# Feed-forward matmuls moved from column tiles to the four quadrants of TensorE, beside attention that already runs there

## The chip, the cores and the metric

One core of one Trainium2 chip. In the profiles PE is TensorE and PEld its weight loads, ACT is ScalarE, DVE VectorE, POOL GpSimd, SP SyncE, and SPq the queue of SP. Results of PE lie in banks of PSUM; an *eviction* is the instruction by which another engine takes one out of there. The metric is the device time of one execution in microseconds (us). A kernel's time is the median of its runs. A ratio of two kernels is computed from the mean time of one kernel's fast runs over the mean time of the other's fast runs of the same rounds, so it is not quite the ratio of the medians that are quoted. "Fast" and "slow" are states of a run: on one core, a run more than 1.5% above the fastest run of the same kernel is called slow.

## The reference

Sigmoid attention over 8 batches, 12 heads, 448 positions and head size 64, then a feed-forward block with SiLU on the 3584 x 768 result (768 to 2048 to 768). Cut to what matters:

```python
scores = scale * np.matmul(q, k.transpose(0, 1, 3, 2)) - np.log(S)
attn = 1.0 / (1.0 + np.exp(-scores))
x = np.matmul(attn, v)            # heads side by side: (8 * 448, 768)
h = x @ w_in                      # 768 -> 2048
g = h * (1.0 / (1.0 + np.exp(-h)))
out = g @ w_out                   # 2048 -> 768
```

## The kernel before

Attention has a contraction of 64 (head size, or 64 keys) and outputs of 64 rows, so it runs in the four 64x64 quadrants of TensorE. One *score step* is four such matmuls of 448 columns, followed by a sigmoid on ACT. The *values* of four heads are 28 of them. The feed-forward products have a contraction of 128 and run as two 128x64 column tiles. I call the matmuls that use the whole array once a *round*: four quadrant matmuls, or two column-tile matmuls. Attention of batch b+1 is woven into the feed-forward stream of batch b, a few score steps at each *visit*. Batch 0 has no feed-forward work to go with it; the last batch's feed-forward work has no attention left.

The parts that matter (cuts marked `# ...`):

```python
ps_sc = ctx.enter_context(tc.tile_pool(name="ps_sc", bufs=2, space=bass.MemoryType.PSUM))  # scores: two pairs of banks
ps_1 = ctx.enter_context(tc.tile_pool(name="ps_1", bufs=4, space=bass.MemoryType.PSUM))    # all else: four single banks

def matmul2(ps, lhsT, rhs, start, stop):          # 128x64 column tiles
    for i in range(2):
        nc.tensor.matmul(ps[half(i)], lhsT[:, half(i)], rhs, start=start, stop=stop)

def scores(b, i, r):                              # 64x64 quadrants
    # ...
    psc = ps_sc.tile([P, 2, 512], F32, tag="pssc", name=f"psc_{b}_{i}_{r}")
    for t in range(2):
        for j in range(2):
            nc.tensor.matmul(
                psc[half(j), t, :S], kT[half(t), r, half(j)], qT[half(t), :, half(j)],
                start=True, stop=True,
            )
    return nc.scalar.activation(attn[b, i][:, :, r, :], psc[:, :, :S], AF.Sigmoid, bias=bias_s, scale=QKSCALE)

def h_unit(b, fc):                                # one 128-row block of h
    # ...
    for cc in range(NCC):
        matmul2(ph[:, :S], w_in_sb[:, cc, fc * P : (fc + 1) * P], xTs[b][:, cc, :], cc == 0, cc == NCC - 1)
    # sigmoid on ACT, product on DVE

# the driver: visits of two or three score steps
while n < len(steps) or waiting:
    now = waiting[:]
    visit = steps[n : n + (3 if now else 2)]
    acts = [scores(*s) for s in visit[:2]]
    for quad in now:
        values(*quad)
    # ...
    gemm(stream_at(n) if n < len(steps) else 1e9 if not waiting else stream_at(n - 0.5))
```

## Time and profile before

| | before |
|---|---|
| median of 3 runs | 401.49 us (401.16 to 403.14) |
| span of the profiled run, granted clock | 399.4 us, 1.00 |
| TensorE (PE) busy | 390.3 us, 98% |
| first feed-forward round starts | 29.1 us |

The first lines of the page of the kernel before follow: busy time by engine, then the span in 40 slices, in tenths busy (PE) and in tenths of the full clock (PEclk), and the chain of waits by engine.

```profile
span 399.4 us, 11191 instructions
PE 390.3 (98%) x5020; PEld 229.7 (58%) x5020; DVE 152.2 (38%) x254; ACT 223.2 (56%) x298; POOL 55.3 (14%) x69
...
PE   8999998999999999999999999999999999999995
...
PEclk9999999999999999999999999999999999999999
...
PE 88%; DMA 9%; POOL 1%; ACT 0%; SPq 0%; issue 0%; DVE 0%; POOLq 0%
```

PE bounds this kernel: it is busy everywhere at full clock, and the chain of waits is 88% PE. But a busy PE is not a PE at its peak. One visit in the timeline of PE shows it (start us, duration us, engine, line, operation, tile, shapes, count; L179 is the score step, L248 the output product):

```profile
162.37 0.38 PE L179 MATMUL psc_2_6_2951<-qT_2_1954,kT_2_1958 64*64 64x448 f16 x4
162.58 0.36 PE L179 MATMUL psc_0_0_2958<-qT_0_2469,kT_0_2473 64*64 64x448 f16 x4
162.87 2.79 PE L248 MATMUL po_0_2969<-w_out_sb,gT_2357 128*64 128x384 f16 x32
165.59 0.38 PE L179 MATMUL psc_0_1_3003<-qT_0_2469,kT_0_2473 64*64 64x448 f16 x4
```

Read the starts, not the durations, because matmuls overlap. The starts of consecutive rounds inside a product are 0.189 us apart with 448 columns and 0.1625 us with 384 columns. The two score steps and 16 output rounds from 162.37 to 165.59 ought to take 2 x 0.189 + 16 x 0.1625 = 2.98 us, and took 3.22. The missing 0.24 us lie at the two borders: 0.10 us going in, 0.10 us coming out, and 0.025 us in the first round after each. The Trainium skill ("TensorEngine Tiling (Array Packing)", Key Properties) says that changing the tiling mode, not just the tile, drains TensorE. This trace agrees: gaps stand where 64x64 and 128x64 tiles meet, and none between score steps and values, which are both 64x64.

Summed over the whole stream, from 29.1 us to PE's end, the rounds take 347.1 us and PE loses 18.2 us: 12.1 us at the borders, 3.1 us in the slower first rounds, 2.0 us in one wait for a DMA, and about 1 us in small pieces.

### The profile page before, as it was taken

Reading aid. Unit: us, or ns where it says so; the run is one execution under the profiler, and the core shown is the slowest. Engines: PE = TensorE matmul, PEld = TensorE weight load, DVE = VectorE, ACT = ScalarE, POOL = GpSimd, SP = SyncE. Lnnn points to the kernel's source line nnn. Section 1 sums busy time; section 2 is a strip of 40 time slices with the busy share of each in tenths; the row PEclk is TensorE's granted clock in tenths of the full one; section 3 lists DMA queues with packets and bytes.
Section 4 is the critical chain, followed back from the end, with each engine's and each line's share of the span. In section 5 each row is a group of like instructions: output and inputs, shape, how many; then the busy total and the mean of one; then the engine's idle time right before and its main releaser. Section 6 shows DMA issues by size and latency. Waiting matters only on the chain.

```text
span 399.4 us, 11191 instructions
## 1 busy us (share of the span) xinstructions
PE 390.3 (98%) x5020; PEld 229.7 (58%) x5020; DVE 152.2 (38%) x254; ACT 223.2 (56%) x298; POOL 55.3 (14%) x69
## 2 busy tenths in 40 slices
PE   8999998999999999999999999999999999999995
PEld 4565554555665556655566555555566555665663
DVE  3544632244323542235322443235421454235411
ACT  2998764477534874566634775467634578214200
POOL 3642020123202110122002120021100000000000
PEclk9999999999999999999999999999999999999999
DMA  7999999699928881595135981396713100130033
GB/s 258 259 252 232 217 218 157 158 172 311 214 56 191 199 178 36 140 240 158 36 80 141 229 173 25 94 217 174 122 41 81 41 2 2 41 80 2 2 80 79
DMA packets 64655, 53.80 MB, mean 135 GB/s; under 512 B 35424, under 2 KB 61024, under 8 KB 64608
## 3 DMA queue, kind: packets, MB, share of 16 engines
q1 hardware_dynamic: 50976, 41.30, 41.5%
q0 software_dynamic: 13632, 11.80, 19.6%
q8 instruction: 39, 0.64, 0.6%
q14 instruction: 8, 0.07, 0.0%
HBM read 45.61 MB, written 11.01 MB: 142 GB/s over the span
## 4 chain that ended last, share of the span: by engine, by line
PE 88%; DMA 9%; POOL 1%; ACT 0%; SPq 0%; issue 0%; DVE 0%; POOLq 0%
DMA kT_0_1135<-xk_0_1133 3%; DMA stk_0_1015<-in_k_dram 2%; DMA v_0_140<-in_v_dram 2%; DMA stk_0_83<-in_k_dram 1%; PE po_0_6030 L248 1%; PE po_0_3461 L248 1%; PE po_1_3055 L248 1%; PE po_0_2869 L248 1%; PE po_0_2748 L248 1%; PE po_1_2321 L248 1%; PE po_0_2147 L248 1%; PE po_0_5909 L248 1%; PE po_0_5788 L248 1%; PE po_1_5393 L248 1%; PE po_1_5259 L248 1%; PE po_0_5225 L248 1%
## 5 line engine op out<-in xcount | busy, mean ns | idle before, releaser
L84 PEld LDWEIGHTS <-w_in_sb 128*64 128x64 f16 x1536 | 84.3, 110 | 63.6 <-issue 10.7
L248 PEld LDWEIGHTS <-gT_3896 128*64 128x64 f16 x224 | 14.0, 110 | 7.7 <-issue 1.8
L248 PEld LDWEIGHTS <-gT_2357 128*64 128x64 f16 x224 | 14.0, 110 | 7.7 <-issue 1.8
L248 PEld LDWEIGHTS <-gT_724 128*64 128x64 f16 x224 | 13.9, 110 | 7.8 <-issue 2.0
L248 PEld LDWEIGHTS <-gT_5429 128*64 128x64 f16 x224 | 14.1, 110 | 7.0 <-issue 0.9
L248 PEld LDWEIGHTS <-gT_1552 128*64 128x64 f16 x224 | 14.0, 110 | 5.8 <-issue 1.4
L248 PEld LDWEIGHTS <-gT_4630 128*64 128x64 f16 x224 | 14.0, 110 | 5.8 <-issue 1.4
L248 PEld LDWEIGHTS <-gT_3091 128*64 128x64 f16 x224 | 14.0, 110 | 5.8 <-issue 1.4
L248 PEld LDWEIGHTS <-gT_6100 128*64 128x64 f16 x224 | 14.4, 110 | 4.7
L92 PEld LDWEIGHTS <-zeros 64*64 64x64 f16 x180 | 6.3, 121 | 4.3 <-issue 1.9
L92 PE MATMUL pz_start<-zeros 64*64 64x448 f16 x44 | 4.3, 577 | 1.2 <-DVE bias_s L67 1.2
L102 POOL DMA_DIRECT2D w_in_sb<-in_moe_w_in_dram x8 | 5.3, 670 | 0.0
L133 POOL DMA_DIRECT2D v_6_3858<-in_v_dram x1 | 0.8, 821 | 27.9 <-PE psc_0_3_3852 L179 27.9
L183 ACT ACTIVATE attnT_0_197<-psc_0_0_198,bias_s 128x896 f16<-128x896 f32 x1 | 1.0, 1007 | 6.3 <-PE psc_0_0_198 L179 6.3
L233 ACT ACTIVATE tsig_0_6114<-ph_0_6101 128x448 f16<-128x448 f32 x1 | 0.5, 545 | 6.9 <-PE ph_0_6101 L84 6.9
L200 PEld LDWEIGHTS <-v_0_140 64*64 64x64 f16 x84 | 2.8, 106 | 2.0 <-DMA v_0_140<-in_v_dram 1.1
L133 POOL DMA_DIRECT2D v_5_3053<-in_v_dram x1 | 0.8, 821 | 22.5 <-PE psc_0_3_3047 L179 22.5
L133 POOL DMA_DIRECT2D v_7_4592<-in_v_dram x1 | 0.8, 821 | 22.5 <-PE psc_0_3_4586 L179 22.5
L183 ACT ACTIVATE attnT_2_5764<-psc_2_4_5926,bias_s 128x896 f16<-128x896 f32 x1 | 1.0, 1008 | 4.5 <-PE psc_2_4_5926 L179 4.5
L183 ACT ACTIVATE attnT_2_4255<-psc_2_4_4425,bias_s 128x896 f16<-128x896 f32 x1 | 1.0, 1007 | 4.5 <-PE psc_2_4_4425 L179 4.5
L183 ACT ACTIVATE attnT_2_3484<-psc_2_4_3673,bias_s 128x896 f16<-128x896 f32 x1 | 1.0, 1008 | 4.5 <-PE psc_2_4_3673 L179 4.5
L183 ACT ACTIVATE attnT_2_2716<-psc_2_4_2886,bias_s 128x896 f16<-128x896 f32 x1 | 1.0, 1007 | 4.5 <-PE psc_2_4_2886 L179 4.5
(1084 smaller groups left out, 986.8 us busy)
## 6 DMA issues: line engine op xcount, KB each, us to landing
w_in_sb<-in_moe_w_in_dram POOLq DMA_DIRECT2D x8, 384.0 KB, 11.3
w_out_sb<-in_moe_w_out_dram POOLq DMA_DIRECT2D x2, 1536.0 KB, 24.4
v_0_140<-in_v_dram POOLq DMA_DIRECT2D x3, 224.0 KB, 7.9
v_1_456<-in_v_dram POOLq DMA_DIRECT2D x1, 672.0 KB, 16.4
v_2_1204<-in_v_dram POOLq DMA_DIRECT2D x1, 672.0 KB, 16.8
v_3_1514<-in_v_dram POOLq DMA_DIRECT2D x1, 672.0 KB, 8.1
v_4_2319<-in_v_dram POOLq DMA_DIRECT2D x1, 672.0 KB, 10.0
v_5_3053<-in_v_dram POOLq DMA_DIRECT2D x1, 672.0 KB, 7.2
```

Source lines behind the costliest of these rows:

```text
L84: nc.tensor.matmul(ps[half(i)], lhsT[:, half(i)], rhs, start=start, stop=stop)
L92: nc.tensor.matmul(pz[j][half(t), :S], zeros[half(j), :D], zeros[half(j)], start=True, stop=True)
L102: nc.gpsimd.dma_start(w_in_sb[half(t), :, f], moe_w_in[t * NCC * D : (t + 1) * NCC * D, f].rearrange("(c d) f -> d c f", d=D),)
L133: nc.gpsimd.dma_start(v16s[b].rearrange("p t i f -> p (t i) f"), src.rearrange("p t i f -> p (t i) f"))
L183: return nc.scalar.activation(attn[b, i][:, :, r, :], psc[:, :, :S], AF.Sigmoid, bias=bias_s, scale=QKSCALE)
L200: nc.tensor.matmul(pav[j][half(t), :S], v16s[b][half(j), t, i, r * D : (r + 1) * D], attnT[half(j), t, r, :], start=(r == 0), stop=(r == R ...
L233: nc.scalar.activation(tsig, ph[:, :S], AF.Sigmoid, bias=0.0, scale=ISX)
L248: nc.tensor.matmul(po[half(s), :NO2], gTs[bl][:, fc, r * D : (r + 1) * D], w_out_sb[:, fc, e], start=(fc == 0), stop=(fc == NFC - 1),)
```

## The change

The intent: run the feed-forward products in the four quadrants too, so that TensorE never changes mode while there is attention to do. A contraction of 128 is then split over the two row halves of the array. Two row halves may not write the same PSUM bank at the same time: the Trainium skill says so ("TensorEngine Tiling (Array Packing)", Gotcha 1: PSUM Pressure). So two products are made at once, in a pair of banks. In the first phase row half 0 adds to bank 0 and row half 1 to bank 1; in the second phase they change over. Between the phases all matmuls of the first must have ended. A no-op on SP's queue waits for them and PE waits for the no-op; one score step is put there to cover the time. The array time of two products stays the same.

PSUM is dealt out anew: one pair of banks for scores (before: two), three pairs for everything else; in batch 0 alone every second score takes a pair of the others. Evictions become twice as wide. The q and k transposes of batches 0 and 1 share one tile. Score steps come one at a time, so there are more, shorter visits.

The diff, cut to its core:

```diff
-    ps_sc = ctx.enter_context(tc.tile_pool(name="ps_sc", bufs=2, space=bass.MemoryType.PSUM))
-    ps_1 = ctx.enter_context(tc.tile_pool(name="ps_1", bufs=4, space=bass.MemoryType.PSUM))
+    ps_sc = ctx.enter_context(tc.tile_pool(name="ps_sc", bufs=1, space=bass.MemoryType.PSUM))
+    ps_2 = ctx.enter_context(tc.tile_pool(name="ps_2", bufs=3, space=bass.MemoryType.PSUM))
 ... (cut)
-    def transpose_pe(b: int, i: int, nm: str, cuts=(0, R)):
+    def transpose_pe(b: int, i: int, cuts=(0, R), between=None):
+        ptr = ps_2.tile([P, 2, 1024], F16, tag="ps2", name=f"ptr_{b}_{i}")
+        for n, nm in enumerate("qk"):
 ... (cut: transposes into ptr[:, n], eviction by DVE)
+    def products(n, nk, lhs, rhs, out_of):
+        if attending[0]:
+            for ph in range(2):
+                for k in range(nk):
+                    for row in range(2):
+                        u = row ^ ph
+                        for c in range(2):
+                            mm = nc.tensor.matmul(
+                                out_of(u)[half(c)],
+                                lhs(u, k, c)[half(row)],
+                                rhs(u, k)[half(row)],
+                                start=(ph == 0 and k == 0),
+                                stop=(ph == 1 and k == nk - 1),
+                            )
+                            if ph == 1 and k == row == c == 0:
+                                tc.add_manual_dep(
+                                    mm.ins, change.ins.name, AFTER, reason="rows change over"
+                                )
+                    if ph == 0 and k == nk - 1:
+                        change = nc.sync.nop()
+                        tc.add_manual_dep(
+                            change.ins, mm.ins.name, AFTER, reason="rows change over"
+                        )
+                        for dma in stores:
+                            dma()
+                        stores.clear()
+                    yield n, (ph * nk + k + 1) / (2 * nk)
+        else:
 ... (cut: 128x64 column tiles as before, for the last batch)
+        if kind == "h":
+            o_pairs, o_done = 0, 0
+            if share == 0.5:
+                attend()          # one score step at the change-over
+            o_quota = min((b + 1) * NQ * R + AHEAD, len(steps) + 1) - done
+        elif share < 1 and (done < len(steps) or waiting or share == 0.5):
+            progress = (o_pairs + share) / len(tiles_of(b))
+            if share == 0.5 or o_done < o_quota * progress - 0.5:
+                attend()          # in output pairs: at the change-over, and wherever behind the quota
+                o_done += 1
```

More of the change, by code (lines that the diff above doesn't have):

```diff
@@ L1 @@
+import itertools
 import math
 from contextlib import ExitStack
+from functools import partial
 import concourse.bass as bass
@@ L79, in half, with ps_tile @@
         return slice(i * D, (i + 1) * D)
-    def matmul2(ps, lhsT, rhs, start, stop):
-        for i in range(2):
-            nc.tensor.matmul(ps[half(i)], lhsT[:, half(i)], rhs, start=start, stop=stop)
+    def ps_tile(name, pool=None, tag="ps2"):
+        return (pool or ps_2).tile([P, 2, 512], F32, tag=tag, name=name)
     def idle(n: int, key: str):
-        pz = [ps_1.tile([P, 512], F32, tag="ps1", name=f"pz{i}_{key}") for i in range(2)]
+        pz = ps_tile(f"pz_{key}")
         for _ in range(n):
@@ L92, in idle @@
                     nc.tensor.matmul(
-                        pz[j][half(t), :S], zeros[half(j), :D], zeros[half(j)], start=True, stop=True
+                        pz[half(t), j, :S], zeros[half(j), :D], zeros[half(j)], start=True, stop=True
                     )
@@ L157, in transpose_dma, with scores @@
         nc.sync.dma_start_transpose(xt, x16s.pop((nm, b, i)).rearrange("p r t d -> p (r t d)"))
-    def transpose_pe(b: int, i: int, nm: str, cuts=(0, R)):
-        xt = new_T(b, i, nm)
-        x16 = x16s.pop((nm, b, i))
-        ptr = ps_1.tile([P, 1024], F16, tag="ps1", name=f"ptr_{b}_{i}_{nm}")
-        for r in range(R):
-            for t in range(2):
-                nc.tensor.transpose(ptr[half(t), r * P : (r + 1) * P], x16[:, r, t], ident)
-        for r0, r1 in zip(cuts, cuts[1:]):
-            nc.vector.tensor_copy(
-                xt[:, r0:r1, :], ptr[:, r0 * P : r1 * P].rearrange("e (r c) -> e r c", c=P)
-            )
-    def scores(b: int, i: int, r: int):
+    def transpose_pe(b: int, i: int, cuts=(0, R), between=None):
+        ptr = ps_2.tile([P, 2, 1024], F16, tag="ps2", name=f"ptr_{b}_{i}")
+        for n, nm in enumerate("qk"):
+            xt = new_T(b, i, nm)
+            x16 = x16s.pop((nm, b, i))
+            for r in range(R):
+                for t in range(2):
+                    nc.tensor.transpose(ptr[half(t), n, r * P : (r + 1) * P], x16[:, r, t], ident)
+            for r0, r1 in zip(cuts, cuts[1:]) if nm == "k" else [(0, R)]:
+                nc.vector.tensor_copy(
+                    xt[:, r0:r1, :],
+                    ptr[:, n, r0 * P : r1 * P].rearrange("e (r c) -> e r c", c=P),
+                )
+            if between is not None and n == 0:
+                between()
+    def scores(b: int, i: int, r: int, pool=None, times: int = 1):
         qT, kT = qkT["q", b, i], qkT["k", b, i]
@@ L175, in scores @@
             attn[b, i] = p2.tile([P, 2, R, S], F16, tag="attnT", name=f"attnT_{b}_{i}")
-        psc = ps_sc.tile([P, 2, 512], F32, tag="pssc", name=f"psc_{b}_{i}_{r}")
-        for t in range(2):
-            for j in range(2):
-                nc.tensor.matmul(
-                    psc[half(j), t, :S], kT[half(t), r, half(j)], qT[half(t), :, half(j)],
-                    start=True, stop=True,
-                )
+        if pool is None:
+            psc = ps_tile(f"psc_{b}_{i}_{r}", ps_sc, "pssc")
+        else:
+            psc = ps_tile(f"psc_{b}_{i}_{r}", pool)
+        for _ in range(times):
+            for t in range(2):
+                for j in range(2):
+                    nc.tensor.matmul(
+                        psc[half(j), t, :S], kT[half(t), r, half(j)], qT[half(t), :, half(j)],
+                        start=True, stop=True,
+                    )
         return nc.scalar.activation(
@@ L191, in values @@
         if r0 == 0:
-            pavs[b, i] = [
-                ps_1.tile([P, 512], F32, tag="ps1", name=f"pav{j}_{b}_{i}") for j in range(2)
-            ]
+            pavs[b, i] = ps_tile(f"pav_{b}_{i}")
         pav = pavs[b, i]
@@ L200, in values @@
                     nc.tensor.matmul(
-                        pav[j][half(t), :S],
+                        pav[half(t), j, :S],
                         v16s[b][half(j), t, i, r * D : (r + 1) * D],
@@ L210, in values @@
             xTs[b] = p2.tile([P, NCC, S], F16, tag="xT", name=f"xT_{b}", bufs=3)
-        for j in range(2):
-            nc.vector.tensor_scalar_mul(xTs[b][:, 2 * i + j, :], pav[j][:, :S], SX)
+        nc.vector.tensor_scalar_mul(xTs[b][:, 2 * i : 2 * i + 2, :], pav[:, :, :S], SX)
         if i == NQ - 1:
@@ L218 @@
     out_rows = out.rearrange("(b p r) e -> b r p e", b=B, r=R)
-    def h_unit(b, fc):
+    attending = [True]
+    def products(n, nk, lhs, rhs, out_of):
[15 more added lines that the diff above has]
+                                    mm.ins, change.ins.name, AFTER, reason="rows change over"
+                                )
+                    if ph == 0 and k == nk - 1:
+                        change = nc.sync.nop()
+                        tc.add_manual_dep(
+                            change.ins, mm.ins.name, AFTER, reason="rows change over"
+                        )
+                        for dma in stores:
+                            dma()
+                        stores.clear()
+                    yield n, (ph * nk + k + 1) / (2 * nk)
+        else:
+            for u in range(2):
+                for k in range(nk):
+                    for c in range(2):
+                        nc.tensor.matmul(
+                            out_of(u)[half(c)], lhs(u, k, c), rhs(u, k),
+                            start=(k == 0), stop=(k == nk - 1),
+                        )
+                    yield n, 1
@@ L221, in h_unit, with h_pair @@
+    def h_pair(b, f2):
         if b not in gTs:
             gTs[b] = p2.tile([P, NFC, S], F16, tag="gT", name=f"gT_{b}")
-        ph = ps_1.tile([P, 512], F32, tag="ps1", name=f"ph_{b}_{fc}")
-        for cc in range(NCC):
-            matmul2(
-                ph[:, :S],
-                w_in_sb[:, cc, fc * P : (fc + 1) * P],
-                xTs[b][:, cc, :],
-                cc == 0,
-                cc == NCC - 1,
-            )
-        tsig = p2.tile([P, S], F16, tag="tsig", name=f"tsig_{b}_{fc}", bufs=3)
@@ L233, in h_unit @@
-        nc.scalar.activation(tsig, ph[:, :S], AF.Sigmoid, bias=0.0, scale=ISX)
-        nc.vector.tensor_mul(gTs[b][:, fc, :], ph[:, :S], tsig)
-    osbs = {}
-    def o_unit(g, nh):
-        if g not in osbs:
-            osbs[g] = p2.tile([P, DMODEL], F32, tag="osb", name=f"osb_{g}", bufs=4)
-        osb = osbs[g]
-        blocks = [divmod(2 * g + s, R) for s in range(2)]
-        e = slice(nh * NO2, (nh + 1) * NO2)
-        po = ps_1.tile([P, 512], F32, tag="ps1", name=f"po_{g}_{nh}")
-        for fc in range(NFC):
-            for s, (bl, r) in enumerate(blocks):
-                nc.tensor.matmul(
-                    po[half(s), :NO2],
-                    gTs[bl][:, fc, r * D : (r + 1) * D],
-                    w_out_sb[:, fc, e],
-                    start=(fc == 0),
-                    stop=(fc == NFC - 1),
-                )
-            if fc == NFC // 2 - 1:
-                yield T_O / 2
-        nc.vector.tensor_scalar_mul(osb[:, e], po[:, :NO2], ISX)
-        if nh == 1:
-            for s, (bl, r) in enumerate(blocks):
-                nc.sync.dma_start(out_rows[bl, r], osb[half(s)])
-            del osbs[g]
-        yield T_O / 2
@@ L264 @@
-    T_H = NCC * 0.187
-    T_O = NFC * 0.160
+        ph = ps_tile(f"ph_{b}_{f2}")
+        yield from products(
+            "h",
+            NCC,
+            lambda u, k, c: w_in_sb[:, k, (2 * f2 + u) * P + c * D : (2 * f2 + u) * P + (c + 1) * D],
+            lambda u, k: xTs[b][:, k, :],
+            lambda u: ph[:, u, :S],
+        )
+        tsig = p2.tile([P, 2, S], F16, tag="tsig", name=f"tsig_{b}_{f2}", bufs=3)
+        nc.scalar.activation(tsig, ph[:, :, :S], AF.Sigmoid, bias=0.0, scale=ISX)
@@ new lines, in h_pair, with o_pair, blocks, lhs @@
+        nc.vector.tensor_mul(gTs[b][:, 2 * f2 : 2 * f2 + 2, :], ph[:, :, :S], tsig)
+    osbs = {}
+    stores = []
+    def o_pair(units):
+        for g, _ in units:
+            if g not in osbs:
+                osbs[g] = p2.tile([P, DMODEL], F32, tag="osb", name=f"osb_{g}", bufs=4)
+        po = ps_tile("po_%d_%d_%d_%d" % (*units[0], *units[1]))
+        def blocks(g):
+            return [divmod(2 * g + s, R) for s in range(2)]
+        def lhs(u, k, c):
+            bl, r = blocks(units[u][0])[c]
+            return gTs[bl][:, k, r * D : (r + 1) * D]
+        yield from products(
+            "o",
+            NFC,
+            lhs,
+            lambda u, k: w_out_sb[:, k, units[u][1] * NO2 : (units[u][1] + 1) * NO2],
+            lambda u: po[:, u, :NO2],
+        )
+        (g0, n0), (g1, n1) = units
+        if g0 == g1:
+            nc.vector.tensor_scalar_mul(
+                osbs[g0].rearrange("p (n e) -> p n e", n=2), po[:, :, :NO2], ISX
+            )
+        else:
+            for u, (g, nh) in enumerate(units):
+                nc.vector.tensor_scalar_mul(
+                    osbs[g][:, nh * NO2 : (nh + 1) * NO2], po[:, u, :NO2], ISX
+                )
+        for g, nh in dict(units).items():
+            if nh == 1:
+                osb = osbs.pop(g)
+                for s, (bl, r) in enumerate(blocks(g)):
+                    store = partial(nc.sync.dma_start, out_rows[bl, r], osb[half(s)])
+                    if attending[0]:
+                        stores.append(store)
+                    else:
+                        store()
@@ L273, in gemm_stream @@
                 yield None
-            for fc in range(NFC):
-                h_unit(b, fc)
-                yield T_H
-            order = [(g, nh) for g in tiles_of(b) for nh in range(2)]
+            for f2 in range(NFC // 2):
+                for s in h_pair(b, f2):
+                    yield *s, b
+            gs = list(tiles_of(b))
             if b == 0:
-                order.sort(key=lambda u: u[1])
-            for g, nh in order:
-                yield from o_unit(g, nh)
-    stream = gemm_stream()
-    clock = [0.0]
-    def gemm(until: float):
-        while clock[0] < until:
-            t = next(stream, None)
-            if t is None:
-                return
-            clock[0] += t
+                todo2 = [[(gs[0], n), (gs[1], n)] for n in range(2)] + [[(gs[2], 0), (gs[2], 1)]]
+            else:
+                todo2 = [[(g, 0), (g, 1)] for g in gs]
+            for units in todo2:
+                for s in o_pair(units):
+                    yield *s, b
+    stream = gemm_stream()
     stage(0, 0, split=True)
@@ L302 @@
     stage(0, 2)
-    transpose_pe(0, 0, "q")
-    idle(1, "first")
-    transpose_pe(0, 0, "k", (0, 2, R))
+    transpose_pe(0, 0, (0, 2, R), between=lambda: idle(1, "first"))
     cast(0, 1, "q", nc.vector)
@@ L311 @@
         for r in range(R):
-            act = scores(0, i, r)
+            n = i * R + r
+            act = scores(0, i, r, ps_2 if n % 2 else None, times=3 if r > 3 or (i, r) < (0, 2) else 1)
             if r == 0 and i > 0:
@@ L317 @@
             elif r == 2:
-                transpose_pe(*nxt, "q")
-            elif r == 3:
-                transpose_pe(*nxt, "k")
+                transpose_pe(*nxt)
                 b2, i2 = (nxt[0], nxt[1] + 1) if nxt[1] + 1 < NQ else (1, 0)
@@ L326 @@
                     load_v(1)
-            else:
-                idle(3, f"{i}_{r}")
             if (i, r) in ((0, 0), (1, 0), (2, 2)):
@@ L335 @@
     steps = [(b, i, r) for b in range(1, B) for i in range(NQ) for r in range(R)]
-    ends = [(0, 0.0)]
-    for b in range(B - 1):
-        ends.append(((b + 1) * NQ * R + 3, ends[-1][1] + NFC * T_H + len(tiles_of(b)) * 2 * T_O))
-    def stream_at(n):
-        for (n0, t0), (n1, t1) in zip(ends, ends[1:]):
-            if n <= n1:
-                break
-        return t0 + (t1 - t0) * (n - n0) / (n1 - n0)
+    casted = []
     def side(b, i, r, act):
@@ L352, in side @@
                 load_w_out(0)
+                cast(1, 2, "q", nc.vector)
+                cast(1, 2, "k", nc.gpsimd)
             if (i, r) == (1, 3):
@@ L355, in side @@
             if r == 3 and i + 1 < NQ:
-                for nm in "qk":
-                    transpose_pe(1, i + 1, nm)
-            if (i, r) == (1, 0):
-                cast(1, 2, "q", nc.vector)
-                cast(1, 2, "k", nc.gpsimd)
+                transpose_pe(1, i + 1)
         if b + 1 < B:
@@ L366, in side @@
                     stage(b + 1, i2, behind=act)
-                if n == (14 if b == 1 else 3) and i2 == 0:
+                if n == (18 if b == 1 else 3) and i2 == 0:
                     load_v(b + 1)
@@ L371, in side, with attend @@
                         cast(b + 1, i2, nm, nc.gpsimd)
-                        transpose_dma(b + 1, i2, nm)
-    waiting = []
-    n = 0
-    while n < len(steps) or waiting:
-        now = waiting[:]
-        visit = steps[n : n + (3 if now else 2)]
-        acts = [scores(*s) for s in visit[:2]]
-        for quad in now:
-            values(*quad)
-            waiting.remove(quad)
-        acts += [scores(*s) for s in visit[2:]]
-        for s, act in zip(visit, acts):
-            if s[2] == R - 1:
-                waiting.append(s[:2])
-            side(*s, act)
-        n += len(visit)
-        gemm(stream_at(n) if n < len(steps) else 1e9 if not waiting else stream_at(n - 0.5))
-    gemm(1e9)
+                    casted.append((done + 3, b + 1, i2))
+        if casted and done >= casted[0][0]:
+            _, b2, i2 = casted.pop(0)
+            for nm in "qk":
+                transpose_dma(b2, i2, nm)
+    count = itertools.count()
+    done = 0
+    waiting = None
+    AHEAD = 2
+    def attend():
+        nonlocal done, waiting
+        if done == len(steps):
+            if waiting:
+                values(*waiting)
+                waiting = None
+            else:
+                idle(1, f"mid_{next(count)}")
+            attending[0] = bool(waiting)
+            return
+        b, i, r = steps[done]
+        done += 1
+        act = scores(b, i, r)
+        if waiting:
+            values(*waiting)
+            waiting = None
+        if r == R - 1:
+            waiting = (b, i)
+        side(b, i, r, act)
+    o_pairs = o_quota = o_done = 0
+    while True:
+        s = next(stream, "end")
+        if s == "end":
+            break
+        if s is None:
+            attend()
+            continue
+        kind, share, b = s
+        if kind == "h":
[6 more added lines that the diff above has]
+            if share == 0.5 or o_done < o_quota * progress - 0.5:
+                attend()
+                o_done += 1
+        else:
+            o_pairs += share == 1
 _INS = ['q', 'k', 'v', 'moe_w_in', 'moe_w_out']
```

## The prediction

> **What bounds it now.** TensorE: the page has it busy 390.3 of 399.4 us, and the chain of waits is 88% PE. In the timeline a round of the array takes 0.189 us (two 128x64 matmuls of 448 columns, or four 64x64 ones), an output round 0.1625 us. Rounds from the first feed-forward product (29.1 us) to PE's end (394.6 us) sum to about 347.5 us; 18 us is lost. The starts of rounds show where: about 60 visits to attention inside the feed-forward stream cost 0.24 us each over the rounds' own time. Entering costs 0.10, leaving 0.10, the first round after each some 0.025 more. That is the change between 128x64 and 64x64 tiles; the Trainium skill ("TensorEngine Tiling (Array Packing)", Key Properties) says that changing the tiling mode drains TensorE, and the trace agrees with those 0.10 us gaps. Sum: about 15 us for switches, 2 to 3 us for other waits.
>
> **Removed.** Nearly all of the 15 us: up to the last batch all products run in 64x64 quadrants. Array time stays the same (four quarter matmuls a round instead of two halves), if PE keeps up with twice the instructions; 47 ns a matmul is shown by the values, the output rounds need 41 ns. Wider evictions save 0.08 us of ACT per pair, off the path.
>
> **Added.**
> 1. About 80 change-overs (8 h pairs and 3 to 4 output pairs in each of 7 batches): PE end -> a no-op on SP -> PE. From the last matmul's start a waiting engine starts after 0.41 us (score to sigmoid), and an engine's end restarts PE 0.05 us later; with the no-op some 0.5 to 0.55 us, against 0.38 us that the last round and the score step cover. Uncovered 0.12 to 0.2 us; where values (1.3 us) or a late score stand there, nothing. About 50 are left: 5 to 9 us.
> 2. Scores have one PSUM pair instead of two after batch 0. One score must wait for the former sigmoid: 0.41 + 1.01 + 0.05 = 1.47 us from score to score. In the h pairs the distance is 2.5 us; in the output pairs the new order puts scores one to nine steps of 0.1625 us apart (in three batches one single step). Laying the order end to end with these durations I get some 30 waits, about 13 us (estimate). Part overlaps with change-overs, which is counted.
> 3. q and k transposes share one PSUM tile: the k transposes now wait for q's eviction (0.62 us plus latencies, about 1 us, five times). Batch 0, paced by ACT at 0.9 us a score, gets 1 to 2 us longer; batch 1 adds 1.5 us.
> 4. SP holds no-ops behind DMA issues (transposes 1.2 to 3.1 us each, loads behind a sigmoid): 0 to 3 us. Last eviction twice as wide: 0.4 us.
>
> **Sum.** -15 -1 (first-round and score waits that vanish) + 7 + 13 + 3 + 2 = +9 us. My spacing estimate is rough and the change looks tuned, so I go lower: 407 us, 80% range 395 to 417. Chances: faster by over 2% 0.12, within 2% 0.53, slower 0.35.
>
> **What would show it.** The 0.10 us gaps gone until the last batch; round starts at 0.189 and 0.1625 us still; PE waits for SP of 0.1 to 0.2 us at h changes; PE waits for ACT before scores among output rounds, longest about 1 us; k transposes waiting for DVE; first feed-forward round at 30 to 31 us.
>
> **What would make it wrong.** Faster: score waits well under 13 us, no-ops taking under 0.1 us. Slower: PE not issuing a matmul every 41 ns (output rounds at 0.189 would cost 20 us), or SP blocked for microseconds at changes.

## The result, and the profile after

| | before | after |
|---|---|---|
| median | 401.33 us (4 runs, 401.16 to 403.14) | 422.33 us (4 runs, 421.37 to 428.02) |
| ratio of the fast runs, after over before | | 1.0513 (95%: 1.0466 to 1.0559) |

The change made the kernel 5% slower. The run profiled with the result fell in the slow state (428.02 us). I therefore profiled the unaltered changed kernel again; that run is fast (421.15 us), and all readings "after" are from it unless I say otherwise. Its page, the same lines as before:

```profile
span 419.2 us, 16700 instructions
PE 387.5 (92%) x7856; PEld 265.9 (63%) x7856; DVE 136.6 (33%) x140; ACT 227.5 (54%) x234; POOL 55.1 (13%) x69
...
PE   7779999597999999999999999999999999999994
...
PEclk9999999879999999999999999999999999999998
...
PE 81%; ACT 7%; DMA 4%; SPq 4%; DVE 2%; issue 1%; POOL 1%; POOLq 0%; ACTq 0%
```

PE has 56% more matmuls, but is busy for less of the span. ACT and SP's queue (SPq) are now in the chain of waits, and in the eighth slice (73 to 84 us) PE is half idle, and the clock falls in that slice and the next; the tenth slice has another gap. What PE waited for is said in the view of waits (who <- for whom: us in total, times, longest us); L251 is the no-op, L193 the sigmoid of the scores, L170 the eviction of the transposes:

```profile
PE psc L189 <- ACT attnT L193: 10.7, 16, 0.9
PE po L238 <- SPq L251: 4.6, 1, 4.6
PE ptr L168 <- DVE qT L170: 4.6, 6, 1.0
PE ph L238 <- SPq L251: 3.2, 2, 2.9
```

None of these lines is in the kernel before, whose longest wait of PE is 1.8 us, for a DMA. Two are worth seeing in the timeline. First the wait for the scores' only bank pair (L189 is a score step, L238 a quadrant product):

```profile
117.03 0.36 PE L189 MATMUL psc<-qT,kT 64*64 64x448 f16 x4
117.22 0.33 PE L238 MATMUL po<-w_out_sb,gT 64*64 64x384 f16 x4
117.45 1.01 ACT L193 ACTIVATE attnT<-psc,bias_s 128x896 f16<-128x896 f32 x1 [0.81 <-PE psc L189]
...
118.50 0.38 PE L189 MATMUL psc<-qT,kT 64*64 64x448 f16 x4 [0.95 <-ACT attnT L193]
```

From one score step to the next pass 118.50 - 117.03 = 1.47 us, because the second needs the banks that the sigmoid is still reading. The schedule had put one round of 0.1625 us between them. (The bracket counts the idle time of PE after the modelled end of the last matmul; by starts, 1.12 us are lost.)

Second, the no-op. PE, then SP's queue at the same time:

```profile
77.45 0.38 PE L189 MATMUL psc<-qT,kT 64*64 64x448 f16 x4
82.39 2.45 PE L238 MATMUL po<-w_out_sb,gT 64*64 64x384 f16 x28 [4.57 <-SPq L251]
84.64 0.58 PE L189 MATMUL psc<-qT,kT 64*64 64x448 f16 x4
85.01 2.83 PE L208 MATMUL pav<-attnT,v 64*64 64x448 f16 x28
```

```profile
73.64 1.07 SPq L126 DMA_DIRECT2D stk<-in_k_dram  x1
74.81 1.22 SPq L159 DMA_TRANSPOSE qT<-xq  x1
76.12 6.17 SPq L159 DMA_TRANSPOSE kT<-xk  x1
```

From 76.12 to 82.29 us SP was issuing one transposing DMA; only then did it come to the no-op behind it in its queue, and PE, which had ended the first phase before 77.45 us and the score step by about 77.8, could start the second phase at 82.39. The 7 rounds that follow take 2.25 us where 7 x 0.1625 = 1.14 are due: the clock is halved from 81.6 to 88.4 us. The Trainium skill ("TensorE: Matmul & The Clock Gate", Part 1) says that the clock falls to one half after an idle window of about 3.4 us. This trace agrees here: an idle stretch of 4.6 us, then half clock for 6.8 us, which costs 3.0 us more (sum over the rounds up to 88.4 us).

The chain of waits shows the second case, where SP was held up by work that waits itself (start us, us, what):

```profile
87.11 7.21 DMA stk<-in_k_dram
...
94.44 0.94 POOL xk L148
95.38 1.12 SPq L159
...
96.55 0.02 SPq L251
...
96.61 0.56 PE ph L238 x5
```

A load, its cast on POOL, the transposing DMA of the cast tile, and behind that the no-op: PE waits 2.9 us for a load that has nothing to do with the product at hand.

In the slow run that came with the result, the two waits for SP were 5.2 and 4.8 us, and the clock fell after both, and once more in the first slices, where PE stood waiting for the first tiles:

```profile
PE   6879999595999999999989999999999999999995
...
PEclk8699999886999999999999999999999999999999
```

So in the one slow run that was profiled, the longer time goes with more half clock and longer waits for SP. Its half clock in the first slices (7.5 to 17.8 us) came amid idle stretches of at most 1.2 us, so one long idle stretch is not all that brings it; what else does stays open.

Where the 19.8 us between the two profiled spans (399.4 and 419.2) went, from the starts of PE's rounds and the spans:

| | us |
|---|---|
| mode changes gone (borders 12.1, first rounds 3.1) | -15.2 |
| one wait for a DMA in the kernel before gone | -2.0 |
| scores waiting for the sigmoid before them (output stage) | +13.7 |
| no-op held up in SP's queue, twice (4.6 + 2.9) | +7.5 |
| half clock after that | +3.0 |
| change-overs as intended, 0.10 us on average in each of 48 h pairs (0.09 in most) and about 0.5 us in all in output pairs | +5.4 |
| batch 0 longer (first feed-forward round at 31.8, was 29.1) | +2.7 |
| k transposes waiting for q's eviction in batch 1 | +1.9 |
| tail: last eviction twice as wide (0.96 us, was 0.56) | +0.4 |
| left in small pieces | about +2 |

### The profile page after: what moved, and what is told of

Read it like the earlier page. It is cut to its first block, busy times and chain, and to the rows that moved or that the text cites. A ratio compares the mean times of both kernels' runs of the same rounds, so it can differ in the third digit from the quotient of the medians.

```text
span 426.1 us, 16700 instructions
## 1 busy us (share of the span) xinstructions
PE 391.8 (92%) x7856; PEld 267.8 (63%) x7856; DVE 136.7 (32%) x140; ACT 227.7 (53%) x234; POOL 55.1 (13%) x69
## 4 chain that ended last, share of the span: by engine, by line
PE 82%; ACT 6%; SPq 5%; DMA 2%; DVE 2%; issue 1%; POOL 0%; POOLq 0%
SPq L159 3%; PE po_0_11_1_4793 L238 1%; PE po_0_18_1_7097 L238 1%; PE po_0_4_1_2489 L238 1%; PE po_0_24_1_8894 L263 1%; PE po_0_27_1_9101 L263 1%; PE po_0_26_1_9032 L263 1%; PE po_0_25_1_8963 L263 1%; PE po_0_20_1_7450 L238 1%; PE po_0_13_1_5146 L238 1%; PE po_0_6_1_2842 L238 1%; PE po_0_8_1_3718 L238 1%; PE po_0_15_1_6022 L238 1%; SPq L126 1%; PE po_0_3_1_2335 L238 1%; PE po_0_10_1_4639 L238 1%
## 5 line engine op out<-in xcount | busy, mean ns | idle before, releaser
L238 PEld LDWEIGHTS <-w_in_sb 64*64 64x64 f16 x2688 | 76.0, 108 | 64.5 <-SPq L251 22.1
L238 PEld LDWEIGHTS <-gT_633 64*64 64x64 f16 x448 | 16.6, 110 | 10.5 <-SPq L251 5.7
L238 PEld LDWEIGHTS <-gT_3028 64*64 64x64 f16 x448 | 17.3, 107 | 3.6
L238 PEld LDWEIGHTS <-gT_5332 64*64 64x64 f16 x448 | 17.3, 107 | 3.6
L263 PEld LDWEIGHTS <-gT_8668 128*64 128x64 f16 x224 | 19.1, 110 | 0.1
L238 PEld LDWEIGHTS <-gT_4113 64*64 64x64 f16 x448 | 16.5, 107 | 3.1 <-SPq L251 0.3
L238 PEld LDWEIGHTS <-gT_1805 64*64 64x64 f16 x448 | 16.5, 107 | 3.1 <-SPq L251 0.3
L238 PEld LDWEIGHTS <-gT_6417 64*64 64x64 f16 x448 | 16.5, 107 | 3.1 <-SPq L251 0.3
L263 PEld LDWEIGHTS <-w_in_sb 128*64 128x64 f16 x192 | 12.5, 110 | 5.8 <-issue 0.3
L238 PEld LDWEIGHTS <-gT_7632 64*64 64x64 f16 x384 | 13.3, 107 | 2.5
L238 PE MATMUL po_0_2_1_1595<-w_out_sb,gT_633 64*64 64x384 f16 x128 | 7.4, 367 | 5.2 <-SPq L251 5.2
L238 PE MATMUL ph_1_1871<-xT_1145,w_in_sb 64*64 64x448 f16 x48 | 3.8, 462 | 4.8 <-SPq L251 4.8
L238 PE MATMUL po_1_1_1_1389<-w_out_sb,gT_633 64*64 64x384 f16 x128 | 6.4, 323 | 0.0
L238 PE MATMUL po_0_15_1_6022<-w_out_sb,gT_5332 64*64 64x384 f16 x128 | 6.4, 322 | 0.0
L238 PE MATMUL po_0_8_1_3718<-w_out_sb,gT_3028 64*64 64x384 f16 x128 | 6.4, 322 | 0.0
L238 PE MATMUL po_0_1_0_1181<-w_out_sb,gT_633 64*64 64x384 f16 x128 | 6.3, 323 | 0.0
L238 PE MATMUL po_0_23_1_8485<-w_out_sb,gT_7632 64*64 64x384 f16 x128 | 6.2, 323 | 0.0
L238 PE MATMUL po_0_22_1_8296<-w_out_sb,gT_7632 64*64 64x384 f16 x128 | 6.2, 323 | 0.0
L238 PE MATMUL po_0_9_1_3921<-w_out_sb,gT_3028 64*64 64x384 f16 x128 | 6.2, 323 | 0.0
L238 PE MATMUL po_0_16_1_6225<-w_out_sb,gT_5332 64*64 64x384 f16 x128 | 6.2, 323 | 0.0
L238 PE MATMUL po_0_7_1_3554<-w_out_sb,gT_3028 64*64 64x384 f16 x128 | 6.1, 323 | 0.0
L238 PE MATMUL po_0_14_1_5858<-w_out_sb,gT_5332 64*64 64x384 f16 x128 | 6.1, 323 | 0.0
## 6 DMA issues: line engine op xcount, KB each, us to landing
v_2_1618<-in_v_dram POOLq DMA_DIRECT2D x1, 672.0 KB, 10.5
```

The lines of the kernel that those rows point to most:

```text
L238: mm = nc.tensor.matmul(out_of(u)[half(c)], lhs(u, k, c)[half(row)], rhs(u, k)[half(row)], start=(ph == 0 and k == 0), stop=(ph == 1 and k ...
L263: nc.tensor.matmul(out_of(u)[half(c)], lhs(u, k, c), rhs(u, k), start=(k == 0), stop=(k == nk - 1),)
```

## The experiments

The theory: the quadrants do save the mode changes, and the time is lost in three waits that came with them and can be mended one by one: the no-op's place in SP's queue, the one bank pair for scores, the shared tile of the transposes. The main rival: the quadrant form is slow by itself (more instructions, change-overs, clock), and the waits would come back elsewhere. The first four kernels ran on one chip. There the kernel before had a median of 402.73 us (7 runs, 400.59 to 405.96). All kernels gave correct results. A gain over the unaltered kernel is a difference of medians; the intervals of the ratios leave it an error of a few us.

### The changed kernel again

No edit.

> The changed kernel unaltered, to have its profile in the fast state (the profiled run on record was 428.0 us, slow, clock 0.969). All theories: 421 to 423 us in fast runs. Theory SP (a no-op of the change-over waits on SP behind a transposing DMA): PE again stands idle for about 5 us twice, somewhere between 60 and 105 us, waiting for SP, and the clock is halved after each. Rival (the idle stretches and the half clock belong to the slow state alone): in a fast run those two waits are not there.

Measured: 422.28 us (421.15 to 425.48), ratio 1.0495 (1.0421 to 1.0569), clock 0.976 to 0.988 in four fast runs. Both waits for SP are there in a fast run, 4.6 and 2.9 us. The first was followed by half clock, the second, shorter one was not; so "after each" held only once. The rival falls: the waits belong to the kernel.

### The no-op on ACT's queue

```diff
-                        change = nc.sync.nop()
+                        change = nc.scalar.nop()
```

> The no-op of the change-over sits on ACT's queue instead of SP's; nothing else is altered, the transposing DMAs stay on SP. Theory SP: the two waits of about 5 us and the half clock after them vanish, 10 to 15 us less than the unaltered kernel, 407 to 412 us; the change-overs of the h pairs still leave about 0.1 us each, since the way PE, other engine, PE is as long. Rival (the change-over itself is dear wherever its no-op is): within 4 us of the unaltered kernel. Rival (half clock comes by itself): the half-clock stretches between 80 and 107 us stay.

Measured: 411.12 us (410.56 to 413.11), ratio 1.0214 (1.0150 to 1.0278), 11.2 us less than the unaltered kernel. The transposing DMAs still stand in SP's queue; no wait for the no-op over 0.4 us remains, and in the profiled run the clock is full up to the tail. The view of waits and the slices:

```profile
PE psc L189 <- ACT attnT L193: 10.6, 15, 0.9
PE ptr L168 <- DVE qT L170: 4.6, 6, 1.0
```

```profile
PE   7779999999999999999999999999999999999994
...
PEclk9999999999999999999999999999999999999999
```

The gain agrees with the 7.5 + 3.0 us in the table above. One transposing issue still takes 4.86 us in this run, but no change-over stands behind it any more. That the half clock followed from these waits is borne out by all traces of fast runs: in the three with the long waits for SP (the unaltered kernel and the next two) it is there, in the three without them it is not, but for the tail. The change-overs in h pairs still leave 0.10 us each by the starts of rounds (5.4 us for the 48, three of which cost 0.26): that is their own price, and it is small. A form in which PE waits for its own matmul without another engine was not run, so the smallest possible price of a change-over stays open.

### Two bank pairs for scores in the output stage

```diff
-        act = scores(b, i, r)
+        act = scores(b, i, r, ps_2 if in_o[0] and done % 2 else None)
 ... (cut)
         kind, share, b = s
+        in_o[0] = kind == "o"
```

> In the output stage every second score takes a bank pair of the other pool, so that a score waits for the sigmoid before the last one. Theory scores (one PSUM pair for scores costs about 12 us of PE waiting for ACT between output rounds): PE waits before scores fall from about 12 us to under 3 us, the kernel gets 8 to 11 us faster, 411 to 414 us. Rival (those waits overlap with others and come back as waits for output pairs, whose pool now also holds scores): under 4 us gained.

Measured: 411.83 us (408.84 to 412.82), ratio 1.0207 (1.0123 to 1.0291), 10.4 us less than the unaltered kernel. The line of score waits falls from 10.7 us to 3.4 us, what remains of it in batch 0; by the starts of rounds, the 13.7 us between output rounds are gone, against about 3 us of new, smaller waits:

```profile
PE po L238 <- SPq L251: 5.0, 1, 5.0
PE ptr L168 <- DVE qT L170: 4.6, 6, 1.0
PE ph L238 <- SPq L251: 3.4, 2, 3.2
PE psc L189 <- ACT attnT L193: 3.4, 5, 0.9
...
PE pav L208 <- DVE osb L311: 1.1, 2, 0.6
```

The rival is right about 1 us: values now wait twice for an output eviction, because scores have taken a pair of the common pool. It is wrong about the rest. In this run the 3.2 us wait for SP, too, was followed by half clock (3.4 us of it).

### A PSUM tile each for q and k transposes

```diff
-        ptr = ps_2.tile([P, 2, 1024], F16, tag="ps2", name=f"ptr_{b}_{i}")
         for n, nm in enumerate("qk"):
+            ptr = ps_2.tile([P, 2, 1024], F16, tag="ps2", name=f"ptr_{b}_{i}_{nm}")
```

> q and k transposes get a PSUM tile each again, as before the change. Theory: the k transposes no longer wait about 1 us for q's eviction, five times; 3 to 5 us less, 417 to 419 us, first feed-forward round 2 to 3 us earlier. Rival (batch 0 is paced by the sigmoids, so these waits cost nothing; what it lost it lost to the clock): under 1.5 us, and the first feed-forward round no earlier than in the unaltered kernel of this call.

Measured: 418.95 us (418.69 to 420.00), ratio 1.0405 (1.0343 to 1.0466), 3.3 us less than the unaltered kernel, at the low end of what was expected. The profiled runs differ by 2.1 us only. The waits for q's eviction are gone; in their place the k transposes wait 1.7 us in all for casts and for other work of DVE, and values once 1.1 us for a load of v. The first feed-forward round starts at 30.2 us instead of 31.8, so 1.6 us earlier, not 2 to 3 (in the two runs before this one, with the same batch 0 as the unaltered kernel, it started at 31.3 and 31.4); the rest came from batch 1. Batch 0 is paced by the sigmoids, but not so tightly that a wait of 1 us in TensorE costs nothing.

### All three edits together

The kernel before had a median of 402.47 us (11 runs, 401.52 to 404.58). It was run at another time.

> The three edits together: no-op of the change-over on ACT, two bank pairs for scores in the output stage, own PSUM tiles for q and k transposes. Theory (three separate losses, each shown alone at about 11, 11 and 3.5 us): they add up, 395 to 399 us, 1 to 2% faster than the kernel before; full clock until the end; left over about 5 us at the change-overs of the h pairs. Rival (they hide behind each other, one mended the next shows): 402 us or more.

Measured: 398.03 us (397.37 to 400.71, 6 runs), ratio 0.9891 (0.9858 to 0.9924). The changed kernel with these edits is 1.1% faster than the kernel before, shown by an interval that excludes 1. The single gains were 11.2 + 10.4 + 3.3 = 24.9 us; together they gave 24.3 (the unaltered kernel was not run again; by the ratios, 1.0495 to 0.9891, it is the same). Within the error of these numbers the losses were separate.

```profile
span 395.6 us, 16700 instructions
PE 382.1 (97%) x7856; PEld 247.4 (63%) x7856; DVE 136.4 (34%) x140; ACT 226.5 (57%) x234; POOL 55.0 (14%) x69
...
PE   7789999999999999999999999999999999999994
...
PEclk9999999999999999999999999999999999999999
```

By the starts of rounds, PE now loses about 13 us in the stream (before: 18.2), 4.9 us of it at the change-overs of h pairs.

### The same in column tiles

The three edits, but `products` always takes the 128x64 form, so there are no change-overs; the order of score steps is the same. Finished rows are stored at once and not at the next change-over.

```diff
-        if attending[0]:
-            for ph in range(2):
 ... (cut: the quadrant form)
-        else:
+        if True:
             for u in range(2):
                 for k in range(nk):
                     for c in range(2):
                         nc.tensor.matmul(
                             out_of(u)[half(c)], lhs(u, k, c), rhs(u, k),
                             start=(k == 0), stop=(k == nk - 1),
                         )
-                    yield n, 1
+                    yield n, (u * nk + k + 1) / (2 * nk) if attending[0] else 1
```

> The three edits, but the feed-forward products in 128x64 column tiles as in the kernel before; the order of score steps is that of the changed kernel, one at a time, and there are no change-overs. Theory (each visit of 64x64 attention between 128x64 products costs 0.24 us): about 147 visits cost 34 to 36 us, the change-overs' 5 us are saved, so 28 to 33 us more than the kernel with the three edits, 424 to 430 us; gaps of 0.10 us at each entry and exit. Rival (the quadrants gain nothing, what the changed kernel saved came from fewer or wider instructions): within 5 us of the kernel with the three edits.

Measured: 424.86 us (424.83 to 424.89), ratio 1.0546 (1.0506 to 1.0585), 26.8 us more than with quadrants, just below the 28 to 33 that I had expected. The same place in the order, first with quadrants, then with column tiles:

```profile
111.87 0.36 PE L189 MATMUL psc<-qT,kT 64*64 64x448 f16 x4
112.06 1.63 PE L238 MATMUL po<-w_out_sb,gT 64*64 64x384 f16 x36
113.52 0.36 PE L189 MATMUL psc<-qT,kT 64*64 64x448 f16 x4
```

```profile
111.13 0.38 PE L189 MATMUL psc<-qT,kT 64*64 64x448 f16 x4
111.44 1.82 PE L236 MATMUL po<-w_out_sb,gT 128*64 128x384 f16 x20
113.19 0.38 PE L189 MATMUL psc<-qT,kT 64*64 64x448 f16 x4
```

In quadrants the score step takes 112.06 - 111.87 = 0.19 us and nine output rounds take 113.52 - 112.06 = 1.46 us = 9 x 0.1625. In column tiles the score step takes 0.31 us, and ten rounds take 1.75 us instead of 1.625. The loss is at both borders of every visit: by the starts of rounds 294 borders cost 32.2 us in this run. So the quadrants do what they were made for, and at one score step a visit they are worth 27 us. In the kernel before, whose visits bring two or three steps, the mode changes cost only 15.2 us, and that is all there was to win.

## Why the prediction was wrong

I predicted 407 us, 395 to 417, and 422.33 came; against the 401.33 us of the kernel before, +5.7 us were forecast, +21 were measured. Point by point:

- **What bounds the kernel; mode changes about 15 us.** Right: 15.2 us by the starts of rounds. The two forms of the mended kernel, 26.8 us apart, confirm the price per visit.
- **Quadrants keep up at 41 ns a matmul.** Right: rounds stay at 0.189 and 0.1625 us with 56% more matmuls.
- **Change-overs, "5 to 9 us".** Right in sum, at the low end: 5.4 us. Each h pair left 0.09 to 0.10 us, a little under the 0.12 to 0.2 expected.
- **One bank pair for scores, "about 13 us".** Right: 13.7 us by starts, in 29 places (some 30 were expected), and 10.4 us came back when a second pair was given.
- **Shared transpose tile, 3 us.** Right, slightly low: 3.3 us came back; batch 0 and the waits in batch 1 together show 4.6 us, not all of it from this. The first feed-forward round came at 31.8 us, later than the 30 to 31 forecast.
- **"SP holds no-ops behind DMA issues (transposes 1.2 to 3.1 us each, loads behind a sigmoid): 0 to 3 us."** This is the step that failed. The mechanism was named, also among what would make the prediction wrong ("SP blocked for microseconds at changes"), but its size in the sum was wrong: 7.5 us of idle time and 3.0 us of half clock after it, 11.2 us when taken away. I had sized it by the issue durations in the trace of before, whose longest is 3.14 us, and the new trace has one of 6.17 us. Of what earlier entries of the queue wait for I had named loads behind a sigmoid alone. The no-op also had to wait for what a transposing DMA before it waited for: in the second case a load of 7.21 us and a cast. And I had left out that an idle TensorE loses its clock, though the Trainium skill's page "TensorE: Matmul & The Clock Gate" says so.
- **"My spacing estimate is rough and the change looks tuned, so I go lower."** The second fault. My own sum was +9 us, and I took off 3.5 us for a reason that is not in any trace. With the sum as it stood, 410.5 us, and 10.5 us in place of the 1.5 or so that it holds for SP, the estimate would have been about 419.5.

What stays open: why one issue of a transposing DMA took 6.17 us. It was no accident of one run: every profile of the new order has one of 4.2 to 6.6 us that starts between 74 and 85 us. In the stretch from 76.0 to 82.3 us the DMA engines were busy 90% or more almost throughout, with loads of q, k and v among others (the output weights were no longer among them: their last load was issued at 37.9 us). No run here takes one of these loads away, so none shows that they are the cause.

## What to carry to other kernels

Before a semaphore hop is put through another engine's queue, list everything that can stand before it there, and what each of these waits for; here the hop cost 0.1 us on a free queue and up to 4.6 us behind other work. When PSUM is dealt out anew, compute the shortest time from one use of a buffer to the next (here 0.41 + 1.01 + 0.05 = 1.47 us) and compare it with the closest spacing in the new order, not with the mean. A change that is slower can hold a gain: the mode changes were really saved, and three small edits, each found in one line of the view of waits, turned 5% slower into 1% faster.

## What the Trainium skill lacked or had wrong

- "TensorEngine Tiling (Array Packing)", Key Properties: it says that a mode change drains TensorE, but not what that costs. Here it is 0.10 us at each border between 64x64 and 128x64 tiles, and 0.025 us more in the first round after it.
- The same page, Gotcha 1: it asks software to keep row tiles apart in a PSUM bank, but gives no price. Here a change-over through another engine's free queue leaves 0.10 us uncovered when one score step of 0.189 us stands in between.
- The same page gives no sustained rate for 64x64 tiles. Here four matmuls of 384 columns, each with its own weights, start every 0.1625 us, 41 ns a matmul, for the whole stream.
- "TensorE: Matmul & The Clock Gate", Part 1: the half clock after an idle window is confirmed (4.6 us idle, then 6.8 us at half clock). At the edge of its window of about 3.4 us the outcome varied: a wait of 2.9 us had no effect, one of 3.2 us and one of 3.3 us (own PSUM tiles) each brought 3.4 us of half clock.
- "DMA: Bandwidth & Descriptors" counts sequencer cycles of a transposing DMA's issue (for earlier generations, beside trn3's), but does not say how long one can hold the issuing engine's queue while the DMA engines are busy. Here an issue of one and the same size took between 1.2 and 6.2 us.
